# The key-value state of a linear-attention layer: fp32r products of high and low parts, or fp32 products in four column tiles

## The chip, the cores and the metric

One core of one Trainium2 chip runs the whole layer. The metric is the device time of one execution in microseconds; the time of a kernel is the median of its runs.

## The reference

The input x has 2048 rows (tokens) of 512. It is normalized, and one branch computes linear attention with 32 heads of 16, the other a gated feed-forward of width 1376; their product is added to x.

```python
qkv = (xn @ wqkv) ...                       # q, k, v: 32 heads of 16
pk = einsum("bhsd,hdf->bhsf", k, w_phi)      # pq likewise from q
phi_k = concatenate([softmax(pk), softmax(-pk)])   # 32 features a head
kv  = einsum("bhsf,bhsd->bhfd", phi_k, v)    # the key-value state
z   = einsum("bhsf->bhf", phi_k)
num = einsum("bhqf,bhfd->bhqd", phi_q, kv)
den = einsum("bhqf,bhf->bhq", phi_q, z) + 1e-6
s = (num / den) @ wo
h = relu(xn @ W_gate) * (xn @ W_up)
out = x + s * silu(h @ W_down)
```

The change concerns the line of kv: for each head a 32 x 16 matrix, summed over all 2048 tokens.

## The kernel before

**Number format.** Nearly all products are made in fp32r, a 4-byte format of lower precision, from split operands: the high part is the operand rounded by a ScalarE copy, the low part is the rest, made by a subtraction on VectorE or POOL. `mm3` adds up three products (low x high, high x low, high x high). Plain fp32 products are made only where the weights of the feature map are folded into the projections (`fold`, tile pfold).

**First phase.** The 2048 tokens are taken in 16 tiles of 128 (`for n in range(N)`). For each, the normalized x is transposed on TensorE (tile pxT, three token tiles ahead), then come the key projection already multiplied with the feature weights (pk, 12 matmuls of 512 columns), the value projection (pv, 12) and, in `query`, a share of the query projection (pq). `exponents` and `features` turn pk into the 1024 features of each token (32 heads x 2 x 16) in the tile ek: VectorE takes the largest and the smallest of each head and subtracts, ScalarE takes exponentials in two halves, VectorE sums, inverts and scales. In the same function the values are split into vhl, with the high and the low 16 values of each head next to each other.

`features_split(n)` splits the features into phl: the high part on ScalarE (128 x 1024), the low part on POOL. For all but the first token tile POOL's queue then issues a transfer that adds the features to zacc, the sum behind z; the features of the first token tile are written into zacc by VectorE.

`kv_products(n)` makes, for each of eight groups of four heads, one matmul: stationary are the 4 x 2 x 16 = 128 columns of high and low values of the four heads, moving the 256 columns of high and low features (128 each). One matmul thus holds all four combinations of the parts, and the products of a head's values with the features of the three other heads beside them. The results accumulate over all token tiles in four PSUM banks, PKV (tile pkv). The products of token tile n are issued two token tiles later, from n = 10 (`LATER`) on three tiles later, so that features and values are long there; the last ones are issued in the feed-forward that follows.

**Tail of the state.** `state()` adds up what stands in PKV: ScalarE copies the columns of the high features out (four copies), VectorE adds those of the low features (four sums), transposes the 128 x 1024 result in blocks of 32 x 32, and four reductions over the pair of high and low values pick each head's own block into kvt. Then kvt is split into high and low parts for the queries.

**Second phase.** For two halves of the tokens the feed-forward runs in 11 slices (pa, pb, pc, pd, with seven products where eight would stand; py), and beside it the queries' features, their products with the state (pnum), and at the end of each half the output projection (pso).

**Order.** Every engine executes in program order, which is written out by hand around a planner: `Clock` keeps a model of each engine's time as the program is built, and takes pieces of side work (splitting the feed-forward's weights in `f_prep`, the queries, spills) when the model says that the engine is free and the inputs are there. Its cost of a matmul is in model cycles:

```python
cost = max(n, 245) + 30
if name == "matmul" and a[2].dtype == F32 and not k.get("is_transpose"):
    cost = n * 3 + 460
```

**Buffers.** SBUF tiles come from three pools: three of 4096 columns in fp32 or less (u8: raw weights, phl, y), eight of 1024 (u4: ek, vhl, zacc, query features, tiles of the tail) and 41 of 512 (u2: everything else). All PSUM tiles share eight banks.

Of the kernel before, what the change touches and what calls it, by code (L numbers as in the profile page):

```python
# [8 lines left out]
F32R = mybir.dt.float32r  # L9
AF = mybir.ActivationFunctionType  # L10
ALU = mybir.AluOpType
AX = mybir.AxisListType

P = 128
S = 2048
D = 512
H = 32
# [45 lines left out]
class Clock:  # L63
# [21 lines left out]
    def issued(self, key, name, a, k):  # L85
        o, ins = a[0], [*a[1:], *k.values()]
        n = max(x.free_size() for x in [o, *ins] if hasattr(x, "free_size"))
        start = max([self.now, *(self.there(x) + 200 for x in ins)])
        if name == "dma_start":
            self.ready[o.name] = start + self.LANDING  # L90
            if key == "gpsimd":
                self.free[key] = max(start, self.free[key]) + self.ISSUE
            return
        cost = self.RATE[key] * n
        if key == "tensor":
            n = o.free_size()
            cost = max(n, 245) + 30
            if name == "matmul" and a[2].dtype == F32 and not k.get("is_transpose"):
                cost = n * 3 + 460
        if name == "reciprocal":  # L100
            cost *= 6
        self.free[key] = max(start, self.free[key]) + self.FIXED[key] + cost
        self.ready[o.name] = self.free[key] + (380 if key == "tensor" else 0)
# [56 lines left out]
def layer_kernel(ctx: ExitStack, tc: tile.TileContext, x, wkT, wqT, wv, wo, wf, cst, out):  # L160
# [6 lines left out]
    def ps(shape=(P, 512), name="ps"):  # L167
        return pp.tile(list(shape), F32, tag="ps", name=name)

    def u8(shape, name, dt=F32):  # L170
        return sb.tile(list(shape), dt, tag="u8", bufs=B8, name=name)

    def u4(shape, name, dt=F32):
        return sb.tile(list(shape), dt, tag="u4", bufs=B4, name=name)
# [10 lines left out]
    def f32(t):  # L185
        return t.bitcast(F32)

    def add(engine, o, a, b, op=ALU.add):
        engine.tensor_tensor(o, a, b, op=op)
# [4 lines left out]
    def split(hi, lo, src, lo_engine=None):  # L194

        nc.scalar.activation(hi, src, AF.Copy)
        add(lo_engine or nc.vector, lo, src, f32(hi), ALU.subtract)
# [15 lines left out]
    def flat(e):  # L213
        return e.rearrange("p h s f -> p (h s f)")

    def groups(e):
        return e.rearrange("p h s f -> p (h s) f")
# [188 lines left out]

    def features(n, e, raised, pv, between):

        vhl = u4((P, H, 2, DH), "vhl", F32R)
        pvg = pv.rearrange("p (h f) -> p h f", f=DH)  # L410
        sm = small(64, "sm", 2)
        if not raised:
            exp_part(e, 0)
        nc.scalar.activation(vhl[:, :, 0, :], pvg, AF.Copy)
        if not raised:
            exp_part(e, 1)
        between()
        add(nc.vector, vhl[:, :, 1, :], pvg, f32(vhl[:, :, 0, :]), ALU.subtract)
        nc.vector.tensor_reduce(sm, groups(e), op=ALU.add, axis=AX.X)
        nc.vector.reciprocal(pv[:, 0:64], sm)  # L420
        VH[n] = vhl
        if n:
            features_scale(n, e, pv)

    def features_scale(n, e, pv):
        phi = e if n else zacc
        nc.vector.tensor_tensor(groups(phi), groups(e), pv[:, 0:64].unsqueeze(2).to_broadcast([P, 64, DH]), op=ALU.mult)
        EK[n] = phi

    def features_split(n):  # L430
        phi = EK.pop(n)
        phl = u8((P, NG, 2, P), "phl", F32R)
        split(phl[:, :, 0, :], phl[:, :, 1, :], flat(phi).rearrange("p (g f) -> p g f", g=NG), nc.gpsimd)
        if n:
            nc.gpsimd.dma_start(zacc, phi, accum_op=ALU.add)
        PHI[n] = phl

    def kv_products(n):
        phl, vhl = PHI.pop(n), VH.pop(n)
        if n == 0:  # L440
            PKV.extend(ps((P, 2, 256), name="pkv") for _ in range(NG // 2))
        for g in range(NG):
            mm(PKV[g // 2][:, g % 2, :], vhl[:, 4 * g:4 * g + 4], phl[:, g, :, :],
               n == 0 and g % 2 == 0, n == N - 1 and g % 2 == 1)


    RAW, FT, WD = {}, {}, {}
# [643 lines left out]
    for n in range(N):  # L1091
        at[0] = n
        if n + 7 < N:
            load_x(n + 7)
        if n == 2:
            preps = pace.add(all_preps(), 0, 3)
        if 1 < n < N - 4:
            norm_apply(n + 4)
        if 0 < n < N - 5:
            norm_scale(n + 5)  # L1100
        if n > 1:
            pk = project(n, WK, "pk")
        if n > LATER:
            kv_products(n - 3)
            pace.pump()
        turned = [turn(n + LEAD)] if 1 < n < N - LEAD else [turn(3)] if n == 1 else []
        pace.pump()
        if turned and turned[0][0] % 2:
            sums_x(turned[0][0])
        pv = project(n, WV, "pv")  # L1110
        pace.pump()
        if n == 0:
            features(0, early, True, pv, lambda: None)
            pk = project(1, WK, "pk")
            norm_stats(4)
            norm_scale(4)
            lo_xt(*turn(2))
            features_scale(0, early, pv)
            norm_stats(5)
            sums_hi(1)  # L1120
            norm_apply(4)
            norm_scale(5)
            early = exponents(pk)
        else:
            if n == 1:
                norm_apply(5)
            features(n, early if n == 1 else exponents(pk), False, pv, lambda: [lo_xt(*t) for t in turned])
            if n == 1:
                features_split(0)
                sums_lo(1)  # L1130
            query(n - 1)
            pace.pump()
            if n == 1:
                lo_xt(*turn(4))
            if n % 2 == 0 and n - 1 < N // 2:
                pace.later(4, lambda n=n: spill_x(n - 1))
        if n + 6 < N:
            norm_stats(n + 6)
        if n % 2 and n + 2 < N:
            sums_hi(n + 2)  # L1140
        if n:
            features_split(n)
        if n % 2 and n + 2 < N:
            sums_lo(n + 2)
        if 2 <= n < LATER:
            kv_products(n - 2)
            pace.pump()
# [16 lines left out]
    def state():  # L1164
        nonlocal kvacc, zB, kvhl
        kv_products(N - 1)

        kvacc = u4((P, NG, P), "kvacc")
        for g2 in range(NG // 2):
            nc.scalar.activation(kvacc[:, 2 * g2:2 * g2 + 2, :], PKV[g2][:, :, :P], AF.Copy)  # L1170
        for g2 in range(NG // 2):
            g = kvacc[:, 2 * g2:2 * g2 + 2, :]
            add(nc.vector, g, PKV[g2][:, :, P:], g)

        kvhl = XT[:, A21].rearrange("p s k (g c) -> p s (k g) c", c=P)
        yield "vector", kvacc
        kvT = u4((P, NG, P), "kvT")
        nc.vector.transpose(kvT.rearrange("p g c -> p (g c)"), kvacc.rearrange("p g c -> p (g c)"))
        kvacc = None

        def own(t):

            return t.rearrange("p (b q) (s c) -> p b (q s) c", q=2, s=2)[:, :, 0:4:3, :]

        def other(t):
            return t.rearrange("p (b q) (s c) -> p b (q s) c", q=2, s=2)[:, :, 1:3, :]
        yield "vector", kvT
        for c in range(4):
            r = slice(32 * c, 32 * c + 32)
            nc.vector.tensor_reduce(own(kvt[r])[:, :, :, DH * c:DH * c + DH],  # L1190
                                    kvT[r, :, 32 * c:32 * c + 32].rearrange("p (b q) (s v) -> p b q v s", q=2, s=2),
                                    op=ALU.add, axis=AX.X)
        yield "scalar", kvt
        nc.scalar.activation(kvhl[:, 0], kvt, AF.Copy)
        nc.scalar.activation(own(kvhl[:, 1]), own(kvt), AF.Copy)
        yield "gpsimd", kvt
        add(nc.gpsimd, other(kvhl[:, 1]), own(kvt), f32(own(kvhl[:, 0])), ALU.subtract)
        zB = small(256, "zB", 1).rearrange("p (d x) -> p d x", d=4)
        while zhl[1].name not in pace.ready:
            yield 1,  # L1200
        for a in range(2):
            yield "tensor", zhl[1]
            p = ps((P, 4, 4, 32), name="pz")
            for i, z in enumerate(zhl[::-1]):
                mm(p.rearrange("p d i x -> p (d i x)"), ones, z[:, a * 512:(a + 1) * 512], i == 0, i == 1)
            for i in range(4):
                r = slice(32 * i, 32 * i + 32)
                nc.scalar.activation(zB[r, :, 32 * a:32 * a + 32], p[r, :, i, :], AF.Copy)
# [172 lines left out]
```

## Time and profile before

| | us |
|---|---|
| median of 3 runs | 563.39 (563.32 to 564.13) |
| the profiled execution, its own time | 562.88 |
| its span on the core | 561.1 |
| TensorE (PE) busy | 555.5 |
| POOL busy | 404.6 |
| VectorE (DVE) busy | 386.2 |
| ScalarE (ACT) busy | 303.1 |

The durations below come from the one profiled execution. Its own time includes 1.8 us outside the span that the profile shows. PE is the row of matmuls, PEld the row of the loads of their stationary operands, SP the engine that issues most transfers. Nearly all operations go through one helper and so carry the same line number; groups are therefore told apart by the names of their tiles, output first. The ends of matmuls are modelled: a matmul's duration is a latency, and following ones overlap it. Its share of the stream is read from the distance of starts.

### The profile page before, as it was taken

Reading aid. Unit: us, or ns where it says so; the run is one execution under the profiler, and the core shown is the slowest. Engines: PE = TensorE matmul, PEld = TensorE weight load, DVE = VectorE, ACT = ScalarE, POOL = GpSimd, SP = SyncE. Lnnn points to the kernel's source line nnn. Section 1 sums busy time; section 2 is a strip of 40 time slices with the busy share of each in tenths; the row PEclk is TensorE's granted clock in tenths of the full one; section 3 lists DMA queues with packets and bytes.
Section 4 is the critical chain, followed back from the end, with each engine's and each line's share of the span. In section 5 each row is a group of like instructions: output and inputs, shape, how many; then the busy total and the mean of one; then the engine's idle time right before and its main releaser. Section 6 shows DMA issues by size and latency. Waiting matters only on the chain.

```text
span 561.1 us, 8197 instructions
## 1 busy us (share of the span) xinstructions
PE 555.5 (99%) x2618; PEld 465.0 (83%) x2618; DVE 386.2 (69%) x584; ACT 303.1 (54%) x543; POOL 404.6 (72%) x347
## 2 busy tenths in 40 slices
PE   8999999999999999999999999999999999999997
PEld 8888888888888888888888888887888888888886
DVE  5978777676657897799963432799883948665323
ACT  3898687765555557456464151235465555644510
POOL 1689987899888487997978333473568786888473
PEclk9999999999999999999999999999999999999999
DMA  8358999855599817979779999991755765559874
GB/s 285 132 157 238 269 270 324 245 153 166 150 304 321 313 61 261 356 266 285 269 250 322 331 388 410 370 396 47 202 187 193 244 206 183 157 179 320 252 210 165
DMA packets 84539, 137.98 MB, mean 246 GB/s; under 512 B 7824, under 2 KB 34320, under 8 KB 83600
## 3 DMA queue, kind: packets, MB, share of 16 engines
q1 hardware_dynamic: 81040, 125.33, 64.7%
q0 software_dynamic: 3312, 12.06, 11.1%
q8 instruction: 21, 0.34, 0.2%
q14 instruction: 22, 0.18, 0.1%
q10 hardware_dynamic: 144, 0.07, 0.0%
HBM read 76.87 MB, written 52.69 MB: 231 GB/s over the span
## 4 chain that ended last, share of the span: by engine, by line
PE 93%; DVE 3%; DMA 2%; issue 0%; SPq 0%; POOL 0%
PE py L59 21%; PE pd L59 10%; PE pa L59 9%; PE pb L59 8%; PE pv L59 8%; PE pk L59 8%; PE pq L59 8%; PE pso L59 8%; PE pc L59 6%; PE pkv L59 3%; PE pnum L59 3%; PE pxT L59 1%; PE pfold L59 1%; DMA pql<-pq 1%; DMA wd<-ws 1%; DVE eq L59 1%
## 5 line engine op out<-in xcount | busy, mean ns | idle before, releaser
L59 PE MATMUL py<-fdh,hl 128*128 128x512 f32 x176 | 68.5, 389 | 0.0
L59 PE MATMUL py<-fdh,hh 128*128 128x512 f32 x176 | 68.5, 389 | 0.0
L59 PE MATMUL py<-fdl,hh 128*128 128x512 f32 x176 | 68.5, 389 | 0.0
L59 PE MATMUL pa<-XT,wa 128*128 128x512 f32 x264 | 67.0, 389 | 0.0
L59 PEld LDWEIGHTS pa<-XT,wa 128*128 128x128 f32 x264 | 49.6, 188 | 10.3
L59 DVE TENSOR_TENSOR y<-py,y 128x512 f32<-128x512 f32 x40 | 27.5, 689 | 36.5 <-PE py L59 36.5
L59 POOL TENSOR_TENSOR phl<-ek,phl 128x1024 fp32r<-128x1024 f32 x15 | 36.1, 2409 | 10.7 <-ACT phl L59 10.7
L59 PE MATMUL pv<-wvh,XT 128*128 128x512 f32 x128 | 43.5, 401 | 0.0
L59 PE MATMUL pk<-wkh,XT 128*128 128x512 f32 x128 | 42.4, 392 | 0.0
L59 POOL TENSOR_TENSOR ez<-eq,zB 128x1024 f32<-128x1024 f32 x16 | 38.5, 2415 | 4.4 <-ACT eq L59 2.0
L59 POOL TENSOR_TENSOR hl<-t,hh 128x512 fp32r<-128x512 f32 x16 | 20.8, 1298 | 27.3 <-ACT hh L59 26.3
L59 PE MATMUL pq<-XT,wqh 128*128 128x512 f32 (+1 forms) x144 | 40.3, 366 | 0.0
L59 PEld LDWEIGHTS py<-fdh,hh 128*128 128x128 f32 x176 | 33.0, 188 | 6.9
L59 PEld LDWEIGHTS py<-fdl,hh 128*128 128x128 f32 x176 | 33.0, 188 | 6.8
L59 PEld LDWEIGHTS py<-fdh,hl 128*128 128x128 f32 x176 | 33.0, 188 | 6.8
L59 POOL TENSOR_TENSOR y<-y,ys 128x512 f32<-128x512 f32 x24 | 30.9, 1291 | 9.6 <-ACT ys L59 9.6
L59 PE MATMUL pd<-XT,wd 128*128 128x512 f32 x132 | 33.8, 390 | 0.5 <-DVE t L59 0.5
L59 PE MATMUL pd<-XT,wc 128*128 128x512 f32 x132 | 33.8, 389 | 0.0
L59 POOL TENSOR_TENSOR ol<-of,oh 128x512 fp32r<-128x512 f32 (+1 forms) x13 | 20.2, 1596 | 18.9 <-ACT oh L59 18.9
L59 PE MATMUL pc<-XT,wb 128*128 128x512 f32 x132 | 33.7, 389 | 0.0
L59 PE MATMUL pb<-XT,wb 128*128 128x512 f32 x132 | 33.5, 389 | 0.0
L59 POOL TENSOR_TENSOR pTl<-ez,pTh 128x1024 fp32r<-128x1024 f32 x10 | 24.0, 2400 | 8.4 <-ACT pTh L59 8.4
(174 smaller groups left out, 1559.2 us busy)
## 6 DMA issues: line engine op xcount, KB each, us to landing
zacc<-ek POOLq DMA_DIRECT2D x15, 512.0 KB, 5.8
xts<-XT SPq DMA_DIRECT2D x4, 1792.0 KB
XT<-xts SPq DMA_DIRECT2D x7, 1024.0 KB, 20.4
wa<-ws SPq DMA_DIRECT2D x26, 256.0 KB, 3.2
wb<-ws SPq DMA_DIRECT2D x26, 256.0 KB, 4.8
wc<-ws SPq DMA_DIRECT2D x26, 256.0 KB, 5.1
ws<-wa SPq DMA_DIRECT2D x22, 256.0 KB, 4.0
ws<-wb SPq DMA_DIRECT2D x22, 256.0 KB, 4.2
```

The costliest lines, as they stand in the source:

```text
L59: return self.tc.keep_in_program_order(op(*a, **k))
```

## The change

- `features`: the values are copied out of PSUM once, by ScalarE, in plain fp32 and in another order (tile v, from the pool of 512 columns). The subtraction that made their low part is gone.
- `features_scale`, `features_split`: no split of the features. The features stay in ek; those of the first token tile go into zacc by a transfer on SP's queue, the others are added by POOL's queue as before.
- `kv_products`: sixteen fp32 matmuls a token tile. Each takes two heads: 2 x 16 columns of values stationary, 2 x 32 columns of features moving, with `tile_position=(0, 32 * c)`, that is all 128 rows and one of four strips of 32 columns of the array. The strip changes with every matmul (`c` is the inner loop). The state is 128 x 256 in one PSUM bank.
- `state`: one copy out of PSUM, no sums, a transpose of 128 x 256, and four copies of each head's own blocks in place of four reductions.
- The planner's cost of such a matmul is `n * 4` model cycles, and on odd token tiles `sums_hi` stands ahead of `norm_stats`, and `sums_lo` ahead of `features_split`. Through the planner's costs other side work moves by some places too: the first weights of the feed-forward are prepared earlier in the first phase.

```diff
-                cost = n * 3 + 460
+                cost = n * 4 if k.get("tile_position") else n * 3 + 460
...
-        vhl = u4((P, H, 2, DH), "vhl", F32R)
-        pvg = pv.rearrange("p (h f) -> p h f", f=DH)
+        v = u2((P, D), "v")
...
-        nc.scalar.activation(vhl[:, :, 0, :], pvg, AF.Copy)
+        nc.scalar.activation(v.rearrange("p (c g f) -> p g c f", c=4, f=DH),
+                             pv.rearrange("p (g c f) -> p g c f", c=4, f=DH), AF.Copy)
...
-        add(nc.vector, vhl[:, :, 1, :], pvg, f32(vhl[:, :, 0, :]), ALU.subtract)
...
-        phi = e if n else zacc
-        nc.vector.tensor_tensor(groups(phi), groups(e), pv[:, 0:64].unsqueeze(2).to_broadcast([P, 64, DH]), op=ALU.mult)
-        EK[n] = phi
+        nc.vector.tensor_tensor(groups(e), groups(e), pv[:, 0:64].unsqueeze(2).to_broadcast([P, 64, DH]), op=ALU.mult)
+        EK[n] = e
...
-        phl = u8((P, NG, 2, P), "phl", F32R)
-        split(phl[:, :, 0, :], phl[:, :, 1, :], flat(phi).rearrange("p (g f) -> p g f", g=NG), nc.gpsimd)
         if n:
-            nc.gpsimd.dma_start(zacc, phi, accum_op=ALU.add)
-        PHI[n] = phl
+            nc.gpsimd.dma_start(zacc, flat(phi), accum_op=ALU.add)
+        else:
+            nc.sync.dma_start(zacc, flat(phi))
+        PHI[n] = phi
...
-        phl, vhl = PHI.pop(n), VH.pop(n)
+        phi, v = PHI.pop(n).rearrange("p (j a c) s f -> p c j a (s f)", a=2, c=4), VH.pop(n)
+        v = v.rearrange("p (c j x) -> p c j x", c=4, j=4)
         if n == 0:
-            PKV.extend(ps((P, 2, 256), name="pkv") for _ in range(NG // 2))
-        for g in range(NG):
-            mm(PKV[g // 2][:, g % 2, :], vhl[:, 4 * g:4 * g + 4], phl[:, g, :, :],
-               n == 0 and g % 2 == 0, n == N - 1 and g % 2 == 1)
+            PKV.append(ps((P, 4, 2, 32), name="pkv"))
+        for j in range(4):
+            for c in range(4):
+                r = slice(32 * c, 32 * c + 32)
+                nc.tensor.matmul(PKV[0][r, j], v[:, c, j], phi[:, c, j], start=n == 0 and j == 0,
+                                 stop=n == N - 1, skip_group_check=True, tile_position=(0, 32 * c))
...
+        if n % 2 and n + 2 < N:
+            sums_hi(n + 2)
         if n + 6 < N:
             norm_stats(n + 6)
         if n % 2 and n + 2 < N:
-            sums_hi(n + 2)
+            sums_lo(n + 2)
         if n:
             features_split(n)
-        if n % 2 and n + 2 < N:
-            sums_lo(n + 2)
...
-        kvacc = u4((P, NG, P), "kvacc")
-        for g2 in range(NG // 2):
-            nc.scalar.activation(kvacc[:, 2 * g2:2 * g2 + 2, :], PKV[g2][:, :, :P], AF.Copy)
-        for g2 in range(NG // 2):
-            g = kvacc[:, 2 * g2:2 * g2 + 2, :]
-            add(nc.vector, g, PKV[g2][:, :, P:], g)
+        kvacc = u2((P, 256), "kvacc")
+        nc.scalar.activation(kvacc, PKV[0].rearrange("p j a f -> p (j a f)"), AF.Copy)
...
-            nc.vector.tensor_reduce(own(kvt[r])[:, :, :, DH * c:DH * c + DH],
-                                    kvT[r, :, 32 * c:32 * c + 32].rearrange("p (b q) (s v) -> p b q v s", q=2, s=2),
-                                    op=ALU.add, axis=AX.X)
+            nc.vector.tensor_copy(own(kvt[r])[:, :, :, DH * c:DH * c + DH], kvT[r, :, 0:4:3, :])
```

More of the change, by code (lines that the diff above doesn't have):

```diff
@@ L417, in features @@
         between()
-        add(nc.vector, vhl[:, :, 1, :], pvg, f32(vhl[:, :, 0, :]), ALU.subtract)
         nc.vector.tensor_reduce(sm, groups(e), op=ALU.add, axis=AX.X)
         nc.vector.reciprocal(pv[:, 0:64], sm)
-        VH[n] = vhl
+        VH[n] = v
         if n:
@@ L1166, in state @@
         kv_products(N - 1)
-        kvacc = u4((P, NG, P), "kvacc")
-        for g2 in range(NG // 2):
-            nc.scalar.activation(kvacc[:, 2 * g2:2 * g2 + 2, :], PKV[g2][:, :, :P], AF.Copy)
-        for g2 in range(NG // 2):
-            g = kvacc[:, 2 * g2:2 * g2 + 2, :]
-            add(nc.vector, g, PKV[g2][:, :, P:], g)
+        kvacc = u2((P, 256), "kvacc")
+        nc.scalar.activation(kvacc, PKV[0].rearrange("p j a f -> p (j a f)"), AF.Copy)
         kvhl = XT[:, A21].rearrange("p s k (g c) -> p s (k g) c", c=P)
         yield "vector", kvacc
-        kvT = u4((P, NG, P), "kvT")
-        nc.vector.transpose(kvT.rearrange("p g c -> p (g c)"), kvacc.rearrange("p g c -> p (g c)"))
+        kvT = u2((P, 256), "kvT")
+        nc.vector.transpose(kvT, kvacc)
+        kvT = kvT.rearrange("p (j x f) -> p j x f", x=4, f=DH)
         kvacc = None
```

## The prediction, made before the changed kernel ran

> **What bounds the kernel now.** I read the page's busy shares first, then the waits of PE, then the chain of waits over a stretch of the first phase, then the views of single tiles.
>
> ```profile
> PE 555.5 (99%) x2618; PEld 465.0 (83%) x2618; DVE 386.2 (69%) x584; ACT 303.1 (54%) x543; POOL 404.6 (72%) x347
> PEclk9999999999999999999999999999999999999999
> ...
> PE 93%; DVE 3%; DMA 2%; issue 0%; SPq 0%; POOL 0%
> ```
>
> TensorE is busy for 99% of the span at the full granted clock in every slice, and 93% of the chain that ended last lies on it. A busy PE is not yet a PE at its peak, so the waits come next.
>
> ```profile
> PE pidle L59 <- DVE mhalf L59: 1.1, 1, 1.1
> PE pxT L59 <- DVE xn L59: 0.5, 1, 0.5
> PE pd L59 <- DVE t L59: 0.5, 1, 0.5
> ```
>
> That is all that PE waits for by name: 2.1 us, of which 1.6 us lie at the start. No wait for features, values or a free bank is among them. So relief of another engine can return 0.5 us at the most, and the change is decided by what it does to PE's own stream. In the chain one token tile looks like this (start, length, work, number of recorded matmuls):
>
> ```profile
> 57.64 0.95 PE pkv L59 x8
> 58.59 2.75 PE pk L59 x12
> 61.34 0.44 PE pxT L59 x4
> 61.78 2.75 PE pv L59 x12
> 64.53 2.72 PE pq L59 x12
> 67.25 0.95 PE pkv L59 x8
> ```
>
> The pieces fill the 9.61 us from one pkv to the next (57.64 to 67.25) without a gap: 0.95 + 2.75 + 0.44 + 2.75 + 2.72 = 9.61. Whatever pkv takes more or less, the token tile takes more or less. Sixteen token tiles pass, and all their pkv groups stand back to back with other PE work:
>
> ```profile
> L59 PE MATMUL pkv<-phl,vhl 128*128 128x256 f32 x128 | 17.7, 282 | 0.0
> L59 PEld LDWEIGHTS pkv<-phl,vhl 128*128 128x128 f32 x128 | 17.3, 191 | 1.1
> ```
>
> The 282 ns is latency of one matmul, not its share of the stream; the share is 0.95 us / 8 = 119 ns.
>
> **The change part by part.**
>
> *Removed from PE.* 128 matmuls of 256 columns: 16 groups of 0.95 us, 15.2 us on the path.
>
> *Added to PE.* 16 matmuls a token tile in plain fp32, 256 in all, with 32 stationary and 64 moving columns each. No matmul in the trace of before is addressed to a part of the array, and none has 64 columns. The nearest rows are the fp32 folds of the weights (16 matmuls in the program for each weight) and, for scale, a 512-column product:
>
> ```profile
> 13.08 1.78 PE pfold L59 x16
> 45.29 2.72 PE pq L59 x12
> ...
> L59 PE MATMUL pfold<-cb,wkT x32: 275/275/322, 6.5 to 10.0; 128*128 128x128 f32 x32
> L59 PE MATMUL pkv<-phl,vhl x128: 277/283/283, 38.2 to 172.0; 128*128 128x256 f32 x128
> L59 PE MATMUL py<-fdh,hl 128*128 128x512 f32 x176 | 68.5, 389 | 0.0
> ```
>
> The first two lines are the chain, the next two are views of one tile (shortest, median and longest duration), the last a group of the page. The fold's weight product wkT has 16 fp32 matmuls in the program and 32 records: an fp32 matmul is two loads and two matmuls on the engine. Each of these, though only 128 columns wide, has the latency of a 256-column product (275 against 283 ns, where 512 columns have 389) and a share of the stream of 1.78 / 16 = 111 ns, against 119 ns for 256 columns and 2.72 / 12 = 227 ns for 512. So each record streams its columns twice, four passes for one fp32 matmul, at (227 - 119) / 256 = 0.42 ns a column and pass, and 4 to 11 ns on top.
>
> A new record then streams 64 columns twice, 128 column passes. Half of a fold's record is 55.6 ns; with the larger extra it is 54 + 11 = 65 ns. A token tile has 32 records: 32 x 55.6 ns = 1.78 us, at most 32 x 65 = 2.08 us, if they go one after another as all matmuls of this trace do. From below the bound is that the four column tiles, which hold different weights and write different partitions, stream at the same time: 8 steps of 55.6 ns, 0.445 us. From above it is that a pair of load and matmul cannot come faster than the fastest pair that this trace shows, 111 ns: 32 x 111 ns = 3.55 us. I take 1.78 us, the value of the row that is nearest in kind (same data type, same two records), because no row shows two matmuls streaming at once. Per token tile that is +0.83 us, and +13.3 us for sixteen.
>
> *A change of tiling, twice a token tile.* The 16 small matmuls stand between products of the full array. If the array must run empty at each change, the cost is what a matmul's latency has beyond its share of the stream: 389 - 227 = 162 ns, twice, sixteen times: 5.2 us. The trace has no such change, so the ends are 0 and 5.2 us; I take 0 in the sum, since alternating shapes (pkv after pq, 256 after 512 columns) leave no gap in the chain above, and keep 5.2 us in the range. The Trainium skill's "TensorEngine Tiling (Array Packing)" (Key Properties) says that a change of the tiling mode, not of the tile alone, drains TensorE; by that rule the sum would carry the 5.2 us. No run so far shows it.
>
> *Removed beside PE.* The split of the features and of the values:
>
> ```profile
> L59 POOL TENSOR_TENSOR phl<-ek,phl 128x1024 fp32r<-128x1024 f32 x15 | 36.1, 2409 | 10.7 <-ACT phl L59 10.7
> L59 ACT ACTIVATE phl<-ek 128x1024 fp32r<-128x1024 f32 x15 | 15.8, 1056 | 9.4 <-DVE ek L59 9.3
> L59 DVE TENSOR_TENSOR vhl<-pv,vhl 128x512 fp32r<-128x512 f32 x16 | 11.1, 691 | 15.6 <-ACT vhl L59 15.6
> L59 ACT ACTIVATE vhl<-pv 128x512 fp32r<-128x512 f32 x16 | 9.5, 596 | 6.9 <-PE pv L59 3.4 <-DMA zacc<-ek 2.2 <-issue 1.2
> ```
>
> POOL loses 36.1 + 2.4 us for the sixteenth tile at the same mean, ACT 15.8 + 1.1 us, DVE 11.1 us. The last line stays as one ScalarE copy of the same 512 elements into another order, counted at the same 596 ns. All of this lies beside PE, which waited for none of it, so it returns nothing. The features reach the products 1056 + 2409 ns earlier; the products of a token tile are issued two tiles (some 19 us) after it, so this was covered and stays so. The tail (one copy out of one PSUM bank instead of four copies and four sums, a shorter transpose) hangs on ScalarE and VectorE, with feed-forward products queued on PE behind the last pkv; zero. Three more PSUM banks go round; PE waited for no bank; zero.
>
> *Added or moved beside PE.* The first token tile's features reach zacc by a transfer on SP's queue instead of by VectorE, and the second tile's accumulating transfer on POOL's queue must wait for it to land. The like transfers:
>
> ```profile
> zacc<-ek POOLq DMA_DIRECT2D x15, 512.0 KB, 5.8
> ...
> 88.50 0.62 ACT L59 ACTIVATE XT<-sa 128x512 fp32r<-128x512 f32 x1
> 94.86 1.58 POOL L59 TENSOR_TENSOR XT<-sa,XT 128x512 fp32r<-128x512 f32 x1
> ```
>
> 5.8 us to landing, against the 9.61 us of a token tile; if the cover fails, POOL stands once for a few us, with the 1/sigma of a later norm behind it, which is due three token tiles on. On odd tiles two ScalarE copies like the 88.50 line move ahead of the norm's sums (1.24 us later, needed three tiles on), and two POOL subtractions like the 94.86 line move ahead of the accumulating transfer (3.2 us later), where a 2.41 us split no longer stands. Zero on PE; without cover at most those 3.2 us, and POOL has more room than before. The features now stay in their 4 KB buffer until their products have run and the values take 2 KB buffers. Waits for such buffers exist already (2.2 us in the vhl line, for zacc) with no idle PE behind them: 0, at most about 2 us.
>
> *Sum.* 562.88 - 15.2 + 28.5 = 576.2 us against the profiled execution's own time (span 561.1, 1.8 us around it). The median of the runs is 0.5 us above that execution; as a median the forecast is 563.39 + 13.3 = **576.7 us**. With the small pair at 65 ns and the emptying at each change it is 563.39 + 18.1 + 5.2 = 586.7 us.
>
> **The rivals.**
>
> *Four column tiles at once (faster).* If matmuls that lie on neighbouring column tiles stream at the same time, and the loop puts the four tiles next to each other, a token tile's products take 0.445 us and the kernel 563.39 - 16 x 0.505 = 555.3 us; with the emptying, 560.5 us. The point of decision is 0.95 us a token tile, a record every 29.7 ns. For it speaks that the tiles share no weights and no outputs; against it, that the two records of an fp32 matmul follow each other on the same tile, and each brings a load. The Trainium skill, "TensorE: Matmul & The Clock Gate" (Part 3, packing small matmuls), has column tiles running concurrently and reports 2.38 times for three tiles of 512 columns; by it this rival would be the likeliest. Nothing in this trace bears it out.
>
> *Overlap of neighbours only.* The second record of a tile waits for the first, but streams beside the first record of the next tile. Then a token tile takes 17 steps of 55.6 ns, 0.945 us: 563.3 us, no change; with the emptying at both ends 568.5 us. This is the natural outcome of in-order matmuls whose pairs share a tile, if there is any overlap at all.
>
> *A pair has a floor.* If load and matmul cannot follow each other faster than 111 ns, a token tile takes 3.55 us, and the kernel 563.39 + 41.6 = 605.0 us; with a floor half way between 55.6 and 111, at 83 ns, it takes 2.66 us and the kernel 590.7 us. For it: no pair in the trace is faster than 111 ns. Against: those pairs all stream 256 column passes, which explain them.
>
> **How the numbers follow.** One after another 0.48, overlap of neighbours 0.25, four at once 0.15, floor 0.12. The range runs from the four-at-once time, rounded down for its own error (554.5), to the half-way floor (591.0): it leaves out half of the floor's 0.12 and some error of the rest. It is wide since the cost of one record is known only between 14 and 111 ns. The likeliest case's own range is 574 to 587. A measurement of this kernel can tell about 0.2% (1.1 us) from no change. Faster: the 0.15, and 0.03 of neighbours overlapping slightly better: 0.18. Within 0.2%: 0.07, overlap without emptying. Slower: 0.75.
>
> **What would show it.** In the profile after, pkv should have 512 records of 64 columns; the chain should show 32 records in some 1.8 us, and one token tile every 10.4 us instead of 9.61. PE's waits should stay near 2 us, POOL should fall by about 38 us, and the time from the last pkv to the end should not change. A pkv group under 0.95 us, or new idle time of PE behind a buffer or zacc, would make the forecast wrong; gaps of some 160 ns at the groups' ends would show the emptying.

## The result, and the profile after

The changed kernel takes 576.81 us (median, 576.1 to 577.37) against 563.36 us before: a ratio of 1.0235, 95% interval 1.0217 to 1.0253. The forecast was 576.7 us. The number fits and the working behind it does not: where nothing held it up PE's stream became shorter, not longer, and the time went into waits that the forecast had put at nothing. The profiled execution took 576.88 us, with a span of 575.1 us.

The page after: busy times, and the granted clock by slices.

```profile
PE 559.1 (97%) x3002; PEld 460.0 (80%) x3002; DVE 372.3 (65%) x564; ACT 287.8 (50%) x524; POOL 366.8 (64%) x331
PEclk9999897999999999999999999999999999999999
```

POOL lost 37.8 us as forecast. PE's share of the span fell from 99 to 97%, and two slices of the first phase have a lower granted clock. What PE waited for (total, times, longest):

```profile
PE pxT L59 <- ACT xn L59: 5.7, 2, 3.4
PE pc L59 <- DVE e L59: 1.5, 1, 1.5
PE pk L59 <- DVE XT L59: 1.4, 1, 1.4
PE pz L59 <- POOL zl L59: 1.4, 1, 1.4
```

These four lines are new: 10.0 us, where before had 2.1 us in all. Now the products. The first lines are one undisturbed token tile in order of time on PE, the last two the view of the tile pkv (shortest, median and longest duration of a record in ns):

```profile
97.81 0.65 PE L59 MATMUL pkv<-ek,v 128*32 128x64 f32 x32
98.39 0.50 PE L59 MATMUL pk<-wkh,XT 128*128 128x512 f32 x1
...
107.27 0.65 PE L59 MATMUL pkv<-ek,v 128*32 128x64 f32 x32
...
L59 PEld LDWEIGHTS pkv<-ek,v x512: 106/110/110, 38.5 to 181.3; 128*32 128x32 f32 x171
L59 PE MATMUL pkv<-ek,v x512: 216/219/244, 38.5 to 181.3; 128*32 128x64 f32 x171
```

There are 512 records, as forecast. But 32 of them, the last with a latency of 0.219 us, fit into 0.65 us: (0.65 - 0.219) / 31 = 13.9 ns a record, 0.445 us a group. That is the price of the rival "four column tiles at once". From one group to the next it is 9.46 us, against 9.61 before; without its old 0.95 us a token tile had 8.66 us, so the new group costs PE 0.80 us, 0.445 for the records and about 0.355 around them.

So where did 13.5 us go? Up to 107 us the distances from group to group are 9.46 us (the first 9.50) except in two places, 13.55 us (57.51 to 71.06) and 17.29 us (80.52 to 97.81): 11.9 us lost there. The first of them on PE:

```profile
57.51 0.65 PE L59 MATMUL pkv<-ek,v 128*32 128x64 f32 x32
...
60.72 0.39 PE L59 MATMUL pk<-wkh,XT 128*128 128x512 f32 x1
63.42 0.66 PE L59 MATMUL pxT<-ident,xn 128*128 128x128 f32 x4 [2.31 <-ACT xn L59]
63.83 0.56 PE L59 MATMUL pv<-wvh,XT 128*128 128x512 f32 x1
...
71.06 0.65 PE L59 MATMUL pkv<-ek,v 128*32 128x64 f32 x32
```

The transposes come 2.5 us late (0.23 us after the last pk would be 60.95), and then pv takes longer, since the granted clock is down. Two stretches, one behind each wait for xn (columns: stretch, length, busy time of PE, PEld, DVE, ACT, POOL, clock, DMA share, GB/s):

```profile
64.00:68.00 4.00, 4.00 (x12) 3.16 (x11) 3.05 (x5) 3.63 (x7) 3.92 (x7) 0.57 1.03 243
88.00:92.00 4.00, 2.98 (x9) 2.57 (x10) 3.50 (x8) 3.78 (x7) 3.79 (x6) 0.50 1.09 343
```

pv runs from 63.83 to 68.25 us here, 4.42 us, and 2.85 us in an undisturbed tile: the clock adds 1.6 us to the wait of 2.5. ScalarE is what xn waited for. Its waits, in order of time, and then SP's queue in the same stretch:

```profile
50.94 0.62 ACT L59 ACTIVATE ek<-ek 128x512 f32<-128x512 f32 x1
58.11 0.60 ACT L59 ACTIVATE v<-pv 128x512 f32<-128x512 f32 x1 [6.55 <-DMA ws<-wb]
...
62.56 0.81 ACT L59 ACTIVATE xn<-xt,lb,lr 128x512 f32<-128x512 f32 x1 [0.35 <-DVE lb L59]
...
81.24 0.60 ACT L59 ACTIVATE xf<-pxT 128x512 f32<-128x512 f32 x1 [7.64 <-PE pkv L59]
```

```profile
43.49 1.25 SPq L59 DMA_DIRECT2D rawg<-wf  x1
54.32 0.33 SPq L59 DMA_DIRECT2D rawd<-wf  x1
54.70 0.42 SPq L59 DMA_DIRECT2D ws<-wb  x1
55.18 0.42 SPq L59 DMA_DIRECT2D ws<-wc  x1
```

The copy of the values needs a 512-column buffer that a spill of prepared weights (ws<-wb) still holds. That spill stands on SP's queue behind rawd, the load of the next slice's raw weights, which waits from 44.7 to 54.3 us for a buffer of its own. SP's waits name the releaser (total, times, longest):

```profile
SPq L59 <- POOL fdl L59: 13.1, 6, 9.5
```

So the buffer is freed by fdl, the last step of the first slice on POOL (start and length; first the kernel before, then the kernel after):

```profile
86.69 1.54 POOL L59 TENSOR_TENSOR fdl<-rawd,fdh 128x512 fp32r<-128x512 f32 x1
```

```profile
52.78 1.51 POOL L59 TENSOR_TENSOR fdl<-rawd,fdh 128x512 fp32r<-128x512 f32 x1
```

The first slice's preparation ends at 54.3 us after and at 88.2 us before: the planner has put it 34 us earlier, and the second slice right behind it. In the second long stretch ScalarE's copy xf waits until the products have run (7.64 us, <-PE pkv); these hold a buffer of the values.

A further 3.2 us are lost behind the two stretches, around the last products and in the feed-forward that follows:

```profile
180.88 0.65 PE L59 MATMUL pkv<-ek,v 128*32 128x64 f32 x32 [0.35 <-DVE one L59]
183.91 1.67 PE L59 MATMUL pc<-XT,wc 128*128 128x512 f32 x6 [1.48 <-DVE e L59]
191.03 0.50 PE L59 MATMUL pz<-zl,ones 128*128 128x512 f32 x1 [1.38 <-POOL zl L59]
```

From the end of the last pkv group to the end of the span it is 393.6 us, 388.8 us before.

### The profile page after: what moved, and what is told of

Read it like the earlier page. It is cut to its first block, busy times and chain, and to the rows that moved or that the text cites. A ratio compares the mean times of both kernels' runs of the same rounds, so it can differ in the third digit from the quotient of the medians.

```text
span 575.1 us, 8915 instructions
## 1 busy us (share of the span) xinstructions
PE 559.1 (97%) x3002; PEld 460.0 (80%) x3002; DVE 372.3 (65%) x564; ACT 287.8 (50%) x524; POOL 366.8 (64%) x331
## 4 chain that ended last, share of the span: by engine, by line
PE 58%; DVE 6%; issue 2%; DMA 1%; ACT 1%; POOL 0%; DVEq 0%; POOLq 0%; ACTq 0%
PE py L59 19%; PE pd L59 8%; PE pa L59 8%; PE pso L59 8%; PE pb L59 8%; PE pc L59 5%; PE pnum L59 3%; DVE eq L59 1%; DVE qs L59 1%; DMA zacc<-ek 1%; DVE mx L59 1%; DVE qd L59 0%; DVE e L59 0%; POOL zl L59 0%; DVE t L59 0%
## 5 line engine op out<-in xcount | busy, mean ns | idle before, releaser
L59 PE MATMUL pv<-wvh,XT 128*128 128x512 f32 x128 | 46.7, 427 | 0.0
L59 DVE TENSOR_REDUCE sm<-ek 128x64 f32<-128x1024 f32 x16 | 19.5, 1220 | 39.9 <-ACT ek L59 39.9
L59 POOL TENSOR_TENSOR XT<-sa,XT 128x512 fp32r<-128x512 f32 x8 | 10.6, 1326 | 35.0 <-ACT XT L59 35.0
```

Source lines behind the costliest of these rows:

```text
L59: return self.tc.keep_in_program_order(op(*a, **k))
```

## The experiments

Two theories stood after this. A: the 512-column buffers are short, because the values moved into that pool. C: the order that the planner made is at fault, with weights prepared too early. B is the forecast's own: the records follow each other in the stream.

**The values in another pool.** Same program order on every engine, one allocation changed.

```diff
-        v = u2((P, D), "v")
+        v = u8((P, 2048), "v")[:, 0:D]
```

> The changed kernel with one edit: the values tile v (2 KB used) is taken from the pool of 2048-column tiles that the split features have left, not from the 41 tiles of 512 columns. The program order of every engine is the same as in the changed kernel. Theory A (buffers): the products themselves have become cheaper (9.46 us a token tile in undisturbed stretches, 9.62 before), and the loss is waits for 512-column buffers that the values hold or wait for: the 2.3 and 3.4 us of PE waiting for xn and the half clock after them go, and the time is 563.4 - 16 x 0.16 = 560.8 us, up to 563 if the waits of the tail (PE for e and zl, 2.9 us) stay. Theory B (the forecast: fp32 records one after another in the stream): the buffers carry nothing, 576.7 us. Theory C (the order that the planner made, weights prepared too early): the order is the same, so 574 to 577 us.

Measured 568.46 us (ratio to before 1.0092, 1.0077 to 1.0107). B falls, and neither A alone (560.8 to 563 us) nor C alone (574 to 577 us) gives this time: 8.4 of the 13.5 us go with the pool. One long stretch stayed, 15.65 us, in which ScalarE's copy of the query projection waits 7.54 us for a spill:

```profile
80.95 0.60 ACT L59 ACTIVATE pqs<-pq 128x512 f32<-128x512 f32 x1 [7.54 <-DMA ws<-wc]
```

**Four matmuls in a row on the same strip.** On top of that kernel:

```diff
-        for j in range(4):
-            for c in range(4):
+        for c in range(4):
+            for j in range(4):
```

> The kernel with v in the other pool, and the two loops of the products exchanged: four matmuls in a row go to the same strip of 32 columns, then the next strip. Same matmuls, same number of records. Theory A: the strips stream at the same time only because neighbours in the program lie on different strips; with four on the same strip a group takes about 16 x 2 x 53 ns less the three overlaps, some 1.6 to 1.8 us instead of 0.45, plus the 0.3 us of changing the tiling, so a token tile is 1.2 to 1.35 us longer and the kernel 560.8 + 19 to 22 = 580 to 583 us. Theory B (order does not matter, the records follow each other anyway): the same time as with the loops as they were.

Measured 576.26 us (1.0231, 1.0216 to 1.0246), 7.8 us more. An undisturbed token tile is 10.21 us, 0.75 us longer:

```profile
102.77 1.39 PE L59 MATMUL pkv<-ek,v 128*32 128x64 f32 x32
```

The records now come every (1.39 - 0.219) / 31 = 37.8 ns in place of 13.9. So it is the change of strip from matmul to matmul that lets them overlap. The starts of single records in the two traces say how. On alternating strips four records start 7, 7 and 6 ns apart and the next four 36 ns later: a step of 56 ns for four. With four matmuls on one strip the starts lie 80, 56, 56 and 56 ns apart, then 6, 50, 30, 26, 30, 26, 30 and 56 ns, which reads as two strips that each take a record every 56 ns, the next strip beginning before the last one is done. That is the 55.6 ns of half a fold's record, and 37.8 ns is the mean of a run that overlaps in part.

The expected 580 us and more were 560.8 us and at least 19 us. This kernel starts from the 568.46 us of the one above, its group takes 1.21 us and not 1.6 (the first term), and less was lost in the long stretch (12.09 in place of 15.65 us).

**The kernel before with a shorter pool.**

```diff
-B8, B4, B2 = 3, 8, 41
+B8, B4, B2 = 3, 8, 39
```

> The kernel before with 39 in place of 41 tiles of 512 columns, nothing else; same program order. Theory A: the pool is the scarce thing, and the four live value tiles took as much from it; with two tiles less the kernel before shows the same kind of waits (ScalarE for a spill or for a late reader, PE for xn) and loses 4 to 14 us: 567 to 577 us. Theory C (only the planner's order hurts): no change, 563.4 us.

Measured 566.39 us (1.0055, 1.0040 to 1.0070), 3.0 us more, with two longer token tiles (10.45 and 11.82 us) in which PE waits for ScalarE's copy pqs. So two buffers less are missed in the kernel before too, but at a lower price than expected.

**Another cost in the planner.**

```diff
-cost = n * 4 if k.get("tile_position") ...
+cost = n * 3 if k.get("tile_position") ...
```

> The changed kernel (values in the 512-column pool) with the planner's cost of a small matmul at n * 3 model cycles in place of n * 4, nearer to the 117 that the trace shows (0.78 us x 2400 / 16). Program orders shift a little. Theory A: the pool is as short as before, waits fall in other places: 570 to 580 us. Theory C: the order was the cause, and the loss falls by a quarter or more of the error in the cost: 566 to 570 us.

Measured 576.21 us (1.0235, 1.0203 to 1.0267), the same time: the first slice still ends at 54.5 us. So this step in the cost, from 256 to 192 model cycles a matmul, does not change the early placing. It leaves a group at 16 x 192 = 3072 model cycles, against 8 x 286 = 2288 for the group of before; a cost as low as the measured one (117 a matmul by the expectation) was not run.

**The old order.** The planner's decisions of the kernel before were recorded (which piece of side work at which of its 673 calls) and replayed in the changed kernel; the hand-moved sums were put back. Once with v in the pool of 2048 columns, once in the pool of 512 columns as in the change:

```diff
-            while self.due(w[0], w[1], w[3]):
-                d = next(w[2], None)
...
+        for made in STEPS.get(self.calls, ()):
+            w = next(w for w in self.work if w[4] == made)
...
```

> The changed kernel with v in the pool of 2048-column tiles, and with every piece of side work (and the sums on odd tiles) at the place where it stands in the kernel before: the planner's decisions of the kernel before are replayed. What is left of the change is the products, the missing splits and the tail. The loss that stayed in values_u8 (one stretch of 15.65 us in place of 9.46, 6.2 us) is put down to the order: weights prepared earlier, whose buffers come free late. If so, no stretch is long any more and the time is 563.4 - 15 x 0.16 = 561 us, below before. If the loss has to do with the products or the missing splits themselves (strips, start of the clock gate, ScalarE's copy of v), it stays near 568 us.

> The same replayed order, but v in the pool of 512-column tiles, as in the changed kernel. Apart from it the loss of the shorter pool: with two tiles less the kernel before lost 3.0 us, and v holds three to four; 564 to 570 us, with waits of ScalarE for spills or for the products. If the pool matters only together with the early preparations: 561 us.

Measured 560.77 us (0.9957, 0.9945 to 0.9970) and 560.94 us (0.9956, 0.9943 to 0.9970). Both beat the kernel before by 2.4 to 2.6 us, and no token tile is long. Two neighbouring groups in the second, and all that PE waits for in it by name:

```profile
58.00 0.65 PE L111 MATMUL pkv<-ek,v 128*32 128x64 f32 x32
67.46 0.65 PE L111 MATMUL pkv<-ek,v 128*32 128x64 f32 x32
...
PE pidle L111 <- DVE mhalf L111: 1.1, 1, 1.1
PE pd L111 <- DVE t L111: 0.5, 1, 0.5
```

With the old order the pool does not matter. Theory A alone falls with this: the values' buffers hurt only together with the early preparation. The waits of pc and pz are gone as well, and from the last pkv group to the end it is 389.4 us.

**The new order in the kernel before.** The other way round: products and splits of before, side work and sums at the changed kernel's places.

> The kernel before, products and splits unchanged, with all side work and the sums at the places where the changed kernel has them (its planner's decisions replayed). If the order by itself costs what stayed in values_u8, 6 to 8 us over 563.4: 569 to 572 us, with PE waiting for xn; POOL and ScalarE carry the splits as well here, so it may be more. If the order needs the shorter pool to hurt: 563 to 565 us.

Measured 594.34 us (1.0548, 1.0532 to 1.0564), far over what was expected: 31 us lost to the order alone. That ScalarE and POOL carry the splits as well here, at a place where the planner had counted on none, fits this but was not tested. ScalarE's longest single wait in the first 200 us is again one for a spill:

```profile
ACT xf L115 <- DMA ws<-wc: 11.9, 1, 11.9
```

**Which part of the order.** First the replayed side work with the sums left where the change has them, then the sums put back with the planner deciding anew.

> The changed kernel with the planner's side work (weights' preparation, spills, queries) at the places of the kernel before, but with the sums of odd token tiles where the changed kernel has them. If the planner's early preparation is the cause, 561 us as in u2_old_order; if the hand-moved sums carry the loss, near 576 us.

> The changed kernel with only the hand-moved lines put back (sums_hi after norm_stats, sums_lo after features_split); the planner decides anew. If the planner's early preparation is the cause, still 572 to 580 us; if the moved sums are, about 561 us.

Measured 560.88 us (0.9956, 0.9941 to 0.9971) and 574.02 us (1.0185, 1.0169 to 1.0201). The side work carries the loss, and the sums carry none of it in the old order. In the second run the planner decides anew, so its 2.8 us under the changed kernel are not the sums' alone: the long distances are others there (11.08, 10.68 and 18.28 us).

**Slower preparation.** Two small edits to the changed kernel, each run alone:

```diff
-            preps = pace.add(all_preps(), 0, 3)
+            preps = pace.add(all_preps(), 0, 1)
```

> The changed kernel with one number of the planner changed: the preparation of weights is taken only while the model sees an engine at most 1 x its limit ahead (3 x before), so that the first weights are prepared over more token tiles. If early preparation is the cause, a good part of the 13 us comes back: 561 to 568 us. If it is not, 575 us.

```diff
         for f in AHEAD:
+            while f == AHEAD[1] and at[0] < 6:
+                yield 3,
             f_load(f)
```

> The changed kernel, planner as it is, with one condition: the raw weights of the second slice that is prepared ahead are not loaded before token tile 6. In the trace of the changed kernel their load stands at 43.5 us on SP's queue and waits there for a buffer until 54.3 us, with the spills of the first slice behind it, for one of which the copy of the values waits. If this queue is the way from early preparation to the lost time, both long stretches shorten and 8 us or more come back: 561 to 568 us. If the buffers alone are short, the wait moves to another instruction and the time stays at 572 to 577 us.

Measured 570.53 us (1.0132, 1.0108 to 1.0156) and 570.69 us (1.0141, 1.0113 to 1.0169): each returns 6 us, about half, less than expected. In both the two long stretches are gone and a later one is there, 20.81 and 17.34 us, where the old order has 12.18. In the second kernel one can see the same jam one slice later, on SP and then on ScalarE:

```profile
84.15 0.61 SPq L59 DMA_DIRECT2D ws<-wc  x1
91.08 0.81 SPq L59 DMA_DIRECT2D rawg<-wf  x2
91.98 0.38 SPq L59 DMA_DIRECT2D rawd<-wf  x1
92.42 0.42 SPq L59 DMA_DIRECT2D ws<-wa  x1
```

```profile
96.93 0.60 ACT L59 ACTIVATE v<-pv 128x512 f32<-128x512 f32 x1 [9.15 <-DMA ws<-wa]
```

**Fewer changes of tiling.** The kernel with v in the other pool and the old order, with the products of two token tiles at once (two values to one buffer, and the like before token tile 10 and at the end):

```diff
         if n > LATER:
-            kv_products(n - 3)
+            if n % 2 == 0:
+                kv_products(n - 4)
+                kv_products(n - 3)
...
```

> The kernel of u8_old_order with the products of two token tiles in a row (three at the end): 8 groups of small matmuls in place of 15, so 7 changes of tiling and back fewer. A group costs 0.78 us of PE's stream for 0.45 us of records; if the 0.32 us on top is paid for each group and not for each record, 7 x 0.32 = 2.3 us are saved: 558.7 us. If it is paid per matmul, no change against u8_old_order.

Measured 558.01 us (0.9905, 0.9891 to 0.9918), the fastest of all: 2.8 us under u8_old_order, 0.39 us for each of the 7 groups saved. Two token tiles take 18.54 us (66.03 to 84.57) in place of 2 x 9.46:

```profile
66.03 1.10 PE L111 MATMUL pkv<-ek,v 128*32 128x64 f32 x64
...
84.57 1.10 PE L111 MATMUL pkv<-ek,v 128*32 128x64 f32 x64
```

The overhead is paid per group.

## Why the prediction was right in its number and wrong in its working

**PE is the bound, and the stream decides: half right.** PE's stream did decide as long as nothing held it up. But "relief of another engine can return 0.5 us at the most" was read as if relief could do no harm. With the change the planner put the side work elsewhere, and that did harm.

**One after another, +13.3 us: wrong.** This is the step that failed: 32 records in a row, 1.78 us a group, "because no row shows two matmuls streaming at once". The price of a record was right, 55.6 ns against a step of 56 ns in the trace; but four strips take their records in the same step. A group's records take 0.445 us, the lower bound, and with what stands around them 0.80 us, less than the 0.95 us of before. The rival "four column tiles at once", which had 0.15, holds: its 555.3 us plus the emptying, 560.5 us, stands against 560.9 us with the old order. Its reading of the Trainium skill ("TensorE: Matmul & The Clock Gate", Part 3, concurrent column tiles) is borne out, 37.8 ns a record on one strip against 13.9 ns on alternating ones. What was held against it, that the two records of one fp32 matmul share a strip, did not stop it.

**No emptying at the change of tiling in the sum: wrong, with the right size as a bound.** The estimate of 0.32 us a group from latency less share stands against 0.355 us from the token tile and 0.39 us from the groups saved. The rule of the Trainium skill's "TensorEngine Tiling (Array Packing)" (Key Properties), that a change of the mode drains TensorE, agrees; the trace shows the price of a group here, though not that it is a drain. The change between fp32r and fp32 alone costs some 0.01 us: in the kernel before the folds of wqT start 0.23 us after the last pk ahead of them (12.69 and 12.92 us), and from the start of the last record of the first folds to the second pk behind them it is 0.35 us, where 0.111 + 0.227 would be 0.34.

**Buffers 0, at most 2 us; tail 0; other side work not priced at all: wrong, and the main error.** The section on the change says that the first weights are prepared earlier; the sum had no term for it. By the runs the place of the side work costs 576.81 - 560.88 = 15.9 us, and the stream returns 2.5. Of the 15.9 the trace after has 11.9 in the two long stretches and 3.2 around the last products and behind them. That the time from the last pkv to the end should not change was a sign that the prediction named; it grew by 4.8 us. The covers named for the moved sums and for zacc held (old_side_work). What is shown: the loss goes with the placing of the side work, and in the first long stretch, as in that of second_slice_late, it comes through a wait for a 512-column buffer whose spill stands behind a load on SP's queue. What is not shown: by which path the second stretch and the 3.2 us come, and which of the planner's inputs makes it early. A cost of the matmul of n * 3 did not change it (planner_n3); the splits that its model no longer sees on ScalarE and POOL are the likely one, which was not run alone.

So the forecast met 576.8 us by luck: +13.3 us for a dearer stream happened to be near -2.5 + 15.9. The chance of 0.75 for slower rested on a stream that the runs do not show; with the old order the change is faster.

One correction to the section on the kernel before: the tiles of the pool u8 hold 2048 columns of fp32 (8 KB), not 4096.

## What to carry to other kernels

When a change takes work off engines whose order comes from a cost model, compare the new program order with the old one before pricing anything, and test the change with the old order replayed. Waiting shows up far from its cause: here a load that waited 9.5 us for a buffer held back every spill behind it on the same queue, and one of these held a buffer that ScalarE's next copy needed. Small matmuls on alternating strips of the array are worth grouping, since each group paid some 0.36 to 0.39 us beyond its records.

## What the runs showed of the hardware that was not expected

- fp32 matmuls of 32 x 64 columns on alternating strips come at 13.9 ns a record, 27.8 ns a matmul, loads of the stationary operand included. In the kernel before the folds' pairs of load and matmul come every 111 ns, and the transposes pxT, the fastest, every 109 ns.
- Such records start in fours, 6 to 7 ns apart, with 56 ns from one four to the next: read by the order of the program, a record takes its strip 56 ns, and the four strips take theirs at once.
- A group of such matmuls between products of the full array costs PE 0.36 to 0.39 us beyond its records.
- Waits of PE of 2.3 and 3.4 us were each followed by some us at a granted clock of 0.5 to 0.57, which added 1.6 us to the first. The waits of 1.4 and 1.5 us between 180 and 192 us were not: the granted clock from 180 to 200 us is 1.00.
